# An attention and token-mixing kernel whose instruction order is written out: one sign operation for the first batch, V's sums on either engine, a third buffer of maxima and a new order

## The chip, the cores and the metric

The kernel runs on one core of one Trainium2 chip. The metric is the device time of one execution in microseconds (us), the median of three runs. A core has five engines with a queue of instructions each: TensorE (PE, its weight loads shown as PEld), VectorE (DVE), ScalarE (ACT), GpSimd (POOL) and SyncE (SP), which here only issues DMAs. An engine works its queue off in order and waits on semaphores for the others.

## What is computed

```python
def _attn_ref(q, k, v, proj):                 # 4 batches, 8 heads, 768 tokens, 64 wide
    q_bits = (np.einsum('bhsd,dk->bhsk', q, proj) > 0)      # 6 signs a token
    k_bits = (np.einsum('bhsd,dk->bhsk', k, proj) > 0)
    mask = bucket(q_bits)[:, :, :, None] == bucket(k_bits)[:, :, None, :]
    scores = np.where(mask, 0.125 * q @ k.T, -1e9)
    attn = np.exp(scores - scores.max(-1, keepdims=True))
    attn = attn / (attn.sum(-1, keepdims=True) + 1e-09)
    return attn @ v

def _moe_ref(x, w_theta, w_tok_r, w_tok_i, w_ch):           # x: heads side by side, 512 wide
    theta = x @ w_theta
    y = w_tok_r @ (x * cos(theta)) + w_tok_i @ (x * sin(theta))     # mixes the 768 tokens
    u = x + y
    return u + np.maximum(u @ w_ch, 0.0)
```

## The kernel before

**Precision.** Almost every product is made of two float16 halves (a high part and a rest), so three matmuls stand for one. The halves are made on the chip: a scale, a high part (mostly ACT), a rest (DVE or POOL).

**Attention.** Heads are prepared in pairs (`prep_qk`, `prep_v`) and worked one at a time. For a pair, `squares` sums q's and k's squares on ACT, six short DVE operations make the two scales (`sc`, lines 515 to 520), `high` and `low` make the halves (`hl`, lines 492 and 498). TensorE multiplies the raw q and k with the projection into one PSUM tile `pb`: rows 0 to 63 are q's, 64 to 127 k's. `sign` turns them into the mask's rows (`rows`, line 543), which DMAs (`bitd`, line 620) put beside the halves in one of three operand sets `qk`. For the very first head there are no such DMAs: copies on ACT, DVE, POOL and SP put the pieces into `qk` (lines 556 to 562), and the first products `sq` need the scaled q and k and all four pieces of `rows` there.

A head then takes two passes. `maxima`: products `sq` (6 tiles of 128 queries), their row maxima on DVE (`mc`, line 660), joined (`mx`), turned by TensorE (`pmx`) and put as one more row of the operands by a DMA of SP (`row`, line 695), with a flag row (`fl` to `ft`, line 700). `step`: products `st` with that row, exp on ACT (`pf`, line 752), a float16 part (`p`, ACT line 758 or POOL line 760) and its rest (POOL, line 764), then the product with V (`po`), a reciprocal and a scaling into `x` (line 824). Eight of the odd heads of batches 2 and 3 take the other way (`turned`: `bt`, `bm`, `late`) with no maxima pass. Odd head 1 of a pair in batch 0 multiplies V in float32 (`vw`).

`prep_v` loads V (`vb`), makes its halves `vv`, and needs the mean of V over all tokens: POOL adds six slices of `vb` into one (lines 401 and 405), and one float32 matmul with a matrix of 1/768 (`mean`) makes the mean in PSUM.

**Token mixing.** `moe` runs for each batch beside the next batch's attention: `ps_th` (theta), cos and sin on ACT, `f` and the halves `z` on DVE, ACT and POOL, `py` (products with the token weights `wtk`), `u`, `ps_r` (the channel product), a ReLU and a final sum (line 1221). The weights are loaded, split and turned on the way (`wf_t`, `wf_th`, `wf_ch`).

**Order.** Nothing is scheduled when the kernel is built. Each step is an `Op` with the engines it may run on (`alts`) and the buffers it takes (`Slot`); two tables written out in the source, `ORDER` (one token for each step: a letter for the engine, P, A, D, G, S, and the step's number) and `SLOTS` (which of a kind's buffers), fix engine, sequence and buffer. A planner outside the kernel made them. The durations in the `alts` and the constants such as `QK0` were the planner's and have no effect here. `beat` (22 steps of two matmuls `pw`) are matmuls without use.

The pool `mc` of row maxima has two buffers. `mc`, `mx`, the row and the flag row of one head share its number. A turned head holds one of these buffers for its own maxima `bm`.

Of the kernel before, what the change touches and what calls it, by code (L numbers as in the profile page):

```python
# [32 lines left out]
def lsh_attention_moe_kernel(ctx: ExitStack, tc: tile.TileContext, q, k, v, proj, w_theta, w_tok_r, w_tok_i, w_ch, out):  # L33
# [6 lines left out]
    P = 128  # L40
# [64 lines left out]
    FREE = dict(ft=2, mc=2, hl=2, rows=2, sc=2, nat=2, vv=2, x=2, z0=1, z1=1, wx=1, wz=1, wf=1, xt=2, xd=2, vw=2, **BUFS)  # L105
# [150 lines left out]
    def prep_weight(src, dst, nm, n, tag, stage, prio, step, by=1.0):  # L256
# [94 lines left out]
    def prep_v(b, hp, prio):  # L351
        t = {}
        full = t["full"] = [b == 0 and (hp, j) in FULL for j in range(2)]
        onpe = False
# [45 lines left out]
        def s1():  # L400
            POOL.tensor_tensor(t["vb"][:, :, 0:3], t["vb"][:, :, 0:3], t["vb"][:, :, 3:6], ALU.add)

        def s2():
            for n in (1, 2):
                POOL.tensor_tensor(t["vb"][:, :, 0], t["vb"][:, :, 0], t["vb"][:, :, n], ALU.add)

        def mean():
            t["pm"] = pm = bank(sm_, [33, 2, D], f"pm_{b}_{hp}")
            if onpe:
                first = True  # L410
                for j in range(2):
                    if full[j]:
                        for n in range(T):
                            mm(pm[:, j], ones1, t["vw"][j][:, n, :D], first, n == T - 1)
                            first = False
                if n_:
                    js = slice(lo_, lo_ + n_)
                    for n in range(2 * T):
                        c0 = 0 if n < T else W1
                        mm(pm[:, js], one33, t["vv"][:, js, n % T, c0 : c0 + D], first, n == 2 * T - 1)  # L420
                        first = False
            else:
                mm(pm, ones33, t["vb"][:, :, 0], True, True)

        def by(r):
            return 1.0 / S if onpe else sc[r]

        def mh():
            t["mh"] = ap_.tile([33, 2, D], F16, tag=f"mh{sv.idx}", bufs=1, name=f"mh_{b}_{hp}")
# [15 lines left out]
        if not onpe:  # L445
            c = op("va1", prio, on("POOL", 970, s1), [c], [svb])
            c = op("va2", prio, on("POOL", 936, s2), [c], [svb])
        d = op("vmean", prio, on("PE", sum(700 if f_ else 380 for f_ in full) if onpe else 220, mean), [c], [svb, sv, sm_] + sw_)
# [184 lines left out]
    def maxima(h, n_, b, G, asm, own=False):  # L633
# [37 lines left out]
        for blk, (lo, hi) in {1: (4, 6), 0: (0, 4)}.items() if own else ((0, (0, T)),):  # L671
            def group(blk=blk, lo=lo, hi=hi):
# [3 lines left out]
                def small(nm_):  # L676
                    return ap_.tile([hi - lo, P], F16, tag=f"{nm_}{lo}_{hi}{smc.tag}", bufs=1, name=f"{nm_}_{nm}_{lo}")
# [638 lines left out]
FOURTHS = ()  # L1316
# [24 lines left out]
    "0000000000000000000000101012021202122001300010000011100100110020001010101103110002111111222033301001011033212201103003130110020311"  # L1341
    "1200111031011101010100011100101010111011132002201003031111030332022010111203032031100131203011010000000033000110011030011001111131"
    "1232103201211010303321211102001031332002021101001311120011101101130000100011130010101001131131100120011113030232020313200332101111"
    "3100311130011020310000000321011000101101111001010010123101000133201131021030012130032112103000103213000213012102320320111300010111"
    "2101010010000111101101010010011313010011213123201200211010113321023020130332112310011010023201031321101010003000021010000011000111"
    "0100012101013123200101323010102320120100113131332112200332010300201132120303201011011131011300111010100111001011013010032013213201"
    "0031000022313320300011101030103203201211102311321011022303000001200013111100011031102331133211000323021101000232102303111001000310"
    "0101200112321023031121110030000111110133010010111020112331111120012230311112300110200133200033032111212102233010121003000013312000"
    "1100010110101011101030030000133200110100123103120323110010121012001033101302110220013103103001111011011311110001111012001112312321"
    "1110132122310000311012200003323111220013003000131102312110220100020003211010110113112222013330200112203000122031102331000000330210"  # L1350
    "0200111112301023011312200201111103101110101001100000233003010110113313221301103301120320101031321031121132200102131003320110211000"
    "3000231101100100210033303010212132011331312012300300201001332101012331001300120120112011031201110210101110001111020022311030000113"
    "1213230030100302330103120112311020101122131300010113221001330010300120103001201030012220111212120111011301222012021031110200011200"
    "0102102001111022011010220211022011022001130110111120012101002011300000001131001211201101003012210102202100030211223002010102111211"
# [206 lines left out]
```

## Time and profile before

| what | value |
|---|---|
| median of 3 runs | 692.23 us (690.75 to 699.36) |
| profiled execution | 687.36 us, its span 685.6 us |
| clock of TensorE granted over the span | 0.999 of full speed |
| busy: PE, PEld | 659.5 us (96%), 389.7 us (57%) |
| busy: DVE, ACT, POOL | 579.1 us (84%), 535.8 us (78%), 457.7 us (67%) |
| DMA | 95.39 MB, mean 139 GB/s |

The profiled execution was shorter than each of the three timed runs; 1.8 us of it lie outside the span. A busy share is a mean over stages: until about 250 us the preparation of weights and of two batches' operands lies beside the attention, after that the mixing's matmuls do.

### The profile page before, as it was taken

The numbers are of one execution on the slowest core, as the hardware profiler recorded it, in microseconds if no ns is written. First come the engines' busy times: TensorE is split into PE (matmuls) and PEld (weight loads), VectorE is DVE, ScalarE is ACT, GpSimd is POOL, SyncE is SP. The second block draws the span as 40 slices with busy tenths as digits, with TensorE's granted clock in tenths as the row PEclk, the third lists the DMA queues.
The fourth block names the chain that finished last, engine by engine and source line by source line (L and its number), as shares of the span: only waits on it lengthen the run. The fifth ranks groups of instructions, "written<-read, shape, count | busy, mean of one in ns | idle before, by whom it ended". The sixth has DMA issues, their size and how long they took to land.

```text
span 685.6 us, 16806 instructions
## 1 busy us (share of the span) xinstructions
PE 659.5 (96%) x6257; PEld 389.7 (57%) x6257; DVE 579.1 (84%) x1236; ACT 535.8 (78%) x947; POOL 457.7 (67%) x453
## 2 busy tenths in 40 slices
PE   7899989899989999999999999999999999999997
PEld 2487776745544556656445565655645565644454
DVE  6999999999999999899988788889978778688121
ACT  5779989999977799999887889998984588873002
POOL 6838857378537668999568778978755898743012
PEclk9999999999999999999999999999999999999999
DMA  6564867677266452579537788989754685880113
GB/s 242 142 170 130 206 165 199 188 156 175 77 170 157 97 111 68 130 197 177 113 82 139 152 167 172 181 210 189 119 105 62 138 173 103 139 177 17 32 29 109
DMA packets 176985, 95.39 MB, mean 139 GB/s; under 512 B 149024, under 2 KB 166792, under 8 KB 176904
## 3 DMA queue, kind: packets, MB, share of 16 engines
q1 hardware_dynamic: 176760, 94.30, 61.4%
q8 instruction: 49, 0.80, 0.5%
q14 instruction: 32, 0.26, 0.2%
q10 hardware_dynamic: 144, 0.03, 0.0%
HBM read 32.53 MB, written 6.29 MB: 57 GB/s over the span
## 4 chain that ended last, share of the span: by engine, by line
PE 64%; DVE 23%; issue 5%; DMA 4%; ACT 2%; POOL 1%; SPq 0%; POOLq 0%; DVEq 0%; ACTq 0%
PE py L82 19%; PE po L82 13%; PE st L82 9%; PE ps_r L82 7%; DVE mc L660 6%; PE ps_th L82 6%; PE sq L82 4%; PE bt L82 4%; DVE f L1164 2%; DMA qk<-row 2%; DVE hl L498 1%; PE pb L82 1%; DVE z L1175 1%; DVE wf_t L244 1%; DVE wf_t L326 1%
## 5 line engine op out<-in xcount | busy, mean ns | idle before, releaser
L764 POOL TENSOR_TENSOR p<-pf,p 128x512 f16<-128x512 f32 x180 | 233.1, 1309 | 73.3 <-ACT p L758 62.9
L82 PE MATMUL py<-z,wtk 128*128 128x512 f16 (+1 forms) x900 | 206.6, 370 | 0.4 <-DVE mt L434 0.2
L660 DVE TENSOR_REDUCE mc<-sq 128x1 f32<-128x512 f32 (+1 forms) x216 | 143.2, 681 | 19.5 <-PE sq L82 18.3
L752 ACT ACTIVATE pf<-st 128x512 f32<-128x512 f32 x216 | 124.9, 592 | 22.0 <-PE st L82 17.5
L82 PEld LDWEIGHTS <-qk 108*128 108x128 f16 (+2 forms) x1056 | 96.1, 99 | 77.7 <-issue 17.7
L82 PEld LDWEIGHTS <-wtk 128*128 128x128 f16 x900 | 85.6, 97 | 89.8 <-issue 3.7
L82 PE MATMUL st<-qk 108*128 108x256 f16 (+1 forms) x576 | 124.9, 326 | 3.9 <-DMA qk<-row 2.3
L918 POOL TENSOR_TENSOR late<-pf,late 128x384 f16<-128x384 f32 x96 | 93.2, 985 | 25.2 <-ACT late L912 20.5
L82 PEld LDWEIGHTS <-p 128*128 128x128 f16 x2160 | 85.7, 97 | 21.5 <-issue 2.5
L758 ACT ACTIVATE p<-pf 128x512 f16<-128x512 f32 x148 | 90.7, 626 | 6.7 <-PE po L82 5.6
L82 PE MATMUL po<-vv,p 128*128 128x65 f16 (+1 forms) x2160 | 93.3, 193 | 0.1
L82 PE MATMUL sq<-qk 108*128 108x256 f16 (+1 forms) x288 | 78.5, 325 | 8.3 <-DVE mc L660 4.0
L904 ACT ACTIVATE pf<-bt,bm 128x384 f32<-128x384 f32 x96 | 60.7, 665 | 21.1 <-DVE bm L892 16.8
L82 PE MATMUL ps_th<-wth,t_x 128*128 128x512 f16 x288 | 68.2, 379 | 1.4 <-DVE z L1130 0.8
L82 PE MATMUL ps_r<-wch,t_u 128*128 128x512 f16 x276 | 68.9, 379 | 0.3 <-DVE wch L298 0.3
L876 DVE TENSOR_REDUCE bm<-bt 128x1 f32<-128x384 f32 x96 | 50.4, 549 | 11.2 <-PE bt L82 10.6
L1218 ACT ACTIVATE rl<-ps_r,qu 128x512 f32<-128x512 f32 x23 | 15.7, 683 | 46.8 <-PE ps_r L82 37.2
L82 PEld LDWEIGHTS <-t_x 128*128 128x128 f16 x288 | 27.4, 97 | 33.0 <-DMA t_x<-s_x 1.8
L1221 POOL TENSOR_TENSOR x<-rl,x 128x512 f32<-128x512 f32 (+1 forms) x9 | 12.0, 1328 | 48.2 <-DVE s_u L1020 32.7
L82 PE MATMUL bt<-qk 108*128 108x384 f16 x192 | 43.3, 327 | 0.0
L82 PEld LDWEIGHTS <-t_u 128*128 128x128 f16 x276 | 25.4, 97 | 26.8 <-issue 1.6
L1164 DVE SCALAR_TENSOR_TENSOR f<-x,zsc,z 128x512 f32<-128x512 f32 x48 | 38.8, 833 | 1.2 <-POOL z L1175 1.1
(177 smaller groups left out, 1084.0 us busy)
## 6 DMA issues: line engine op xcount, KB each, us to landing
qk<-hl SPq DMA_DIRECT2D x62, 192.0 KB
raw<-in_q_dram SPq DMA_DIRECT2D x16, 384.0 KB
raw<-in_k_dram SPq DMA_DIRECT2D x16, 384.0 KB
vb<-in_v_dram SPq DMA_DIRECT2D x16, 384.0 KB
qk<-hl SPq DMA_DIRECT2D x62, 96.0 KB
out_dram<-x SPq DMA_DIRECT2D x23, 256.0 KB
w_t<-in_moe_w_tok_r_dram SPq DMA_DIRECT2D x6, 768.0 KB
w_t<-in_moe_w_tok_i_dram SPq DMA_DIRECT2D x6, 768.0 KB
```

Source lines behind the costliest of these rows:

```text
L82: PE.matmul(out_, l, r, start=start, stop=stop, skip_group_check=True)
L244: return lambda: eng.tensor_tensor(t["f"][:, part], t["f"][:, part], t["sg"][:, part], ALU.mult)
L660: DVE.tensor_reduce(col()[:, cs], u["sq"], AX.X, ALU.max)
L752: ACT.activation(wide("pf", spf, F32), u["st"], AF.Exp, scale=1.0 / (UNIT * math.sqrt(D)))
L758: ACT.activation(o_, u["pf"], AF.Copy)
L764: return lambda: eng.tensor_tensor(wide("p2", sp2, F16), u["pf"], u["p1"], ALU.subtract)
L876: DVE.tensor_reduce(part(y), w["w"], AX.X, ALU.max)
L904: ACT.activation(w["f"], w["w"], AF.Exp, bias=part(4), scale=part(3))
L918: return lambda: eng.tensor_tensor(dst(1), w["f"], dst(0), ALU.subtract)
L1164: DVE.scalar_tensor_tensor(u["f"], tl[b][:, tt], zsc[:, b : b + 1], t["zw"][r][:, tt], ALU.mult, ALU.mult)
L1218: ACT.activation(v_["r"][:, ds_], r_["ps"][:, ds_], AF.Relu, scale=t["qu"][:, to : to + 1])
L1221: return lambda: eng.tensor_tensor(tl[b][:, to, ds_], v_["r"][:, ds_], tl[b][:, to, ds_], ALU.add)
```

## The change

- `FOURTHS = (0,)`: in batch 0 `sign` is one DVE operation on 128 partitions in place of two on 64. The `rows` tile then holds q's and k's rows below each other, and the copies to the operand sets take four DMAs of 12 rows (`bits`, line 595 of the new kernel) in place of two that took q's and k's together (`pairs`).
- V's sums are one step with two choices: POOL as before, or one `tensor_reduce` on DVE over the six slices into a tile `va` of its own. The new `ORDER` takes DVE for 10 of the 16 pairs.
- A third buffer for the maxima (`mc=3`). The small row tiles of the first head share their buffers with the later ones of the same number; `mh` has one buffer in place of two.
- The sums over a weight matrix (`total`) multiply with bfloat16 ones in place of float32 ones (two matmuls of one column).
- `ones` and `one33`, which nothing needs any more, and code for another way of V's mean that was never taken are gone.
- `ORDER` and `SLOTS` are new. Both orders hold the same matmuls, but for the two above. The planner's own assumption on the length of weight loads and its random shifts stand in no line of the kernel but these tables.

```diff
-    FREE = dict(ft=2, mc=2, hl=2, rows=2, sc=2, nat=2, vv=2, x=2, z0=1, z1=1, wx=1, wz=1, wf=1, xt=2, xd=2, vw=2, **BUFS)
+    FREE = dict(ft=2, mc=3, hl=2, rows=2, sc=2, nat=2, vv=2, x=2, z0=1, z1=1, wx=1, wz=1, wf=1, xt=2, xd=2, vw=2, **BUFS)
...
-            mm(u["pa"], ones, col, True, True)
+            mm(u["pa"], onesb, col.bitcast(BF16)[:, 1:2], True, True)
...
-        def s1():
+        def sums():
             POOL.tensor_tensor(t["vb"][:, :, 0:3], t["vb"][:, :, 0:3], t["vb"][:, :, 3:6], ALU.add)
-
-        def s2():
             for n in (1, 2):
                 POOL.tensor_tensor(t["vb"][:, :, 0], t["vb"][:, :, 0], t["vb"][:, :, n], ALU.add)
 
+        def reduced():
+            t["va"] = ap_.tile([P, 2, D], F32, tag="va" + svb.tag, bufs=1, name=f"va_{b}_{hp}")
+            DVE.tensor_reduce(t["va"], t["vb"].rearrange("p h t d -> p h d t"), AX.X, ALU.add)
+
...
-                mm(pm, ones33, t["vb"][:, :, 0], True, True)
+            mm(pm, ones33, t["va"] if "va" in t else t["vb"][:, :, 0], True, True)
...
-            t["mh"] = ap_.tile([33, 2, D], F16, tag=f"mh{sv.idx}", bufs=1, name=f"mh_{b}_{hp}")
+            t["mh"] = ap_.tile([33, 2, D], F16, tag="mh", bufs=1, name=f"mh_{b}_{hp}")
...
-            c = op("va1", prio, on("POOL", 970, s1), [c], [svb])
-            c = op("va2", prio, on("POOL", 936, s2), [c], [svb])
+        c = op("va", prio, {"POOL": (1906, sums), "DVE": (860, reduced)}, [c], [svb])
...
-                    return ap_.tile([hi - lo, P], F16, tag=f"{nm_}{lo}_{hi}{smc.tag}", bufs=1, name=f"{nm_}_{nm}_{lo}")
+                    return ap_.tile([hi - lo, P], F16, tag=f"{nm_}{lo}{smc.tag}", bufs=1, name=f"{nm_}_{nm}_{lo}")
...
-FOURTHS = ()
+FOURTHS = (0,)
...
-S66 S68 P0 So P3 Am S3c Pg S6t Pb A67 Dn P6k A69 D6a D6b Pj D6l P4 P2 D6c S6q A6o Pd G6n D6d D6e D6f Ph D6s S6r A6g Pi Pe D6p A6i P9 D6h Pf
+S68 S66 Pl S6t S3c Pb Am So P3 Pi Dn A69 P6k A67 A6u D6a P2 D6b D6c D6d D6e D6f D6l P6v A6i Pj D6s P1 S86 A6g Pa G6n D6w D6r Pe G6q A6m D6x
```

How the start of the program stands in two queues. ACT's rows from its first squares to the last copy for the first head, before (`raw` are q and k, `vb` is V, `qk` the first operand set; lines 487 and 380 are squares, 492 the high parts, 558 copies):

```order
L487 ACTIVATE hl_0_176,sc_0_177<-raw_0_0_155 128x768
L487 ACTIVATE hl_0_176,sc_0_177<-raw_0_0_157 128x768
L558 ACTIVATE qk_141<-rows_0_191 12x384
L492 ACTIVATE hl_0_176<-raw_0_0_155,sc_0_177 128x768
L492 ACTIVATE hl_0_176<-raw_0_0_157,sc_0_177 128x768
L558 ACTIVATE qk_141<-raw_0_0_155,sc_0_177 64x768
L380 ACTIVATE vv_121,vs_0_227<-vb_0_172 128x12x64
```

The same of ACT now:

```order
L467 ACTIVATE hl_0_174,sc_0_175<-raw_0_0_151 128x768
L467 ACTIVATE hl_0_174,sc_0_175<-raw_0_0_153 128x768
L374 ACTIVATE vv_117,vs_0_183<-vb_0_158 128x12x64
L472 ACTIVATE hl_0_174<-raw_0_0_151,sc_0_175 128x768
L472 ACTIVATE hl_0_174<-raw_0_0_153,sc_0_175 128x768
L538 ACTIVATE qk_137<-raw_0_0_153,sc_0_175 64x768
L538 ACTIVATE qk_137<-raw_0_0_151,sc_0_175 64x768
L538 ACTIVATE qk_137<-hl_0_174 64x768
```

The copy of `rows` has left ACT, V's squares stand before the high parts, and both scaled copies of 64 rows are here now. SP's first loads go with it: V's is the third now and was the sixth.

DVE's rows from the scales of q and k to the first maxima, before:

```order
L515 TENSOR_SCALAR sc_0_177<-sc_0_177 128x1
L516 RECIPROCAL sc_0_177<-sc_0_177 128x1
L543 TENSOR_SCALAR rows_0_191<-pb_0_181,pp 64x384 x2
L517 TENSOR_SCALAR sc_0_177<-sc_0_177 128x1
L518 TENSOR_SCALAR sc_0_177<-sc_0_177 128x1
L519 TENSOR_SCALAR sc_0_177<-sc_0_177 128x1
L520 TENSOR_SCALAR sc_0_177<-sc_0_177 128x2
L562 TENSOR_SCALAR qk_141<-raw_0_0_157,sc_0_177 32x768
L562 TENSOR_SCALAR qk_141<-raw_0_0_157,sc_0_177 64x768
```

The same of DVE now:

```order
L495 TENSOR_SCALAR sc_0_175<-sc_0_175 128x1
L496 RECIPROCAL sc_0_175<-sc_0_175 128x1
L497 TENSOR_SCALAR sc_0_175<-sc_0_175 128x1
L498 TENSOR_SCALAR sc_0_175<-sc_0_175 128x1
L499 TENSOR_SCALAR sc_0_175<-sc_0_175 128x1
L500 TENSOR_SCALAR sc_0_175<-sc_0_175 128x2
L523 TENSOR_SCALAR rows_0_193<-pb_0_177,pp 128x384
L542 TENSOR_SCALAR qk_137<-raw_0_0_151,sc_0_175 32x768
L190 TENSOR_SCALAR vsc<-pa_0_195 128x1
L540 COPY qk_137<-rows_0_193 12x384
```

The scales stand before the signs now; the signs are one row in place of two, and the 64-row copy has gone to ACT.

SP's rows around the second head's row of maxima in batch 0 (head 1), before:

```order
L606 DMA qk_143<-hl_1_279 64x2x768
L607 DMA qk_143<-hl_1_279 64x2x768
L609 DMA qk_143<-hl_1_279 32x2x768 x2
L620 DMA qk_143<-rows_1_475 12x2x384 x2
L695 DMA qk_142<-row_1_0_561 1x6x128
L700 DMA ft_86<-fl_1_0_563 1x6x128 x2
```

The same place of SP now:

```order
L586 DMA qk_139<-hl_1_284 64x2x768
L587 DMA qk_139<-hl_1_284 64x2x768
L589 DMA qk_139<-hl_1_284 32x2x768 x2
L595 DMA qk_139<-rows_1_358 12x384 x4
L675 DMA qk_138<-row_1_0_551 1x6x128
L680 DMA ft_86<-fl_1_0_560 1x6x128 x2
```

Ahead of the row of maxima (line 675) stand four issues for the signs, which were two. This is so seven times in batch 0.

## Rows read from the trace of the kernel before

**Rows 1.** The page: part 1 (busy, instructions), part 4 (chain by engine).

```profile
PE 659.5 (96%) x6257; PEld 389.7 (57%) x6257; DVE 579.1 (84%) x1236; ACT 535.8 (78%) x947; POOL 457.7 (67%) x453
PE 64%; DVE 23%; issue 5%; DMA 4%; ACT 2%; POOL 1%; SPq 0%; POOLq 0%; DVEq 0%; ACTq 0%
```

**Rows 2.** Busy time by stretch: stretch, its length, engines (instructions), clock, DMA share, GB/s.

```profile
0.00:25.00 25.00, 19.78 (x123) 8.78 (x124) 18.56 (x52) 14.84 (x26) 17.44 (x41) 1.00 0.64 205
25.00:125.00 100.00, 94.93 (x1000) 70.68 (x996) 96.06 (x204) 87.65 (x162) 65.39 (x60) 1.00 0.64 165
125.00:250.00 125.00, 116.97 (x1076) 66.19 (x1076) 123.34 (x235) 109.82 (x196) 80.07 (x63) 1.00 0.60 147
250.00:660.00 410.00, 406.52 (x3917) 229.82 (x3916) 333.67 (x735) 319.25 (x560) 288.82 (x286) 1.00 0.64 129
660.00:686.00 26.00, 21.26 (x150) 14.18 (x147) 7.43 (x14) 4.25 (x8) 5.98 (x5) 0.97 0.33 91
```

**Rows 3.** The chain that ended last: start, length, what.

```profile
618.58 23.96 PE py L82 x111
```

**Rows 4.** Timeline of the first 14 us: start, length, engine, line, operation, what it waited for.

```profile
3.08 0.48 SPq L368 DMA_DIRECT2D vb<-in_v_dram  x1
...
5.83 0.19 ACT L487 ACTIVATION_READ_ACCUMULATOR hl<-raw 128x1 f32 x1
...
6.19 1.39 DVE L543 TENSOR_SCALAR rows<-pb,pp 64x384 f16<-64x384 f32 x2 [0.75 <-PE pb L82]
...
7.60 1.71 SPq L556 DMA_DIRECT2D qk<-rows  x2
7.61 0.21 DVE L517 TENSOR_SCALAR sc<-sc 128x1 f32<-128x1 f32 x1
...
7.96 0.50 POOL L560 COPY qk<-rows 12x384 f16<-12x384 f16 x1
...
8.23 0.25 DVE L520 TENSOR_SCALAR sc<-sc 128x2 f32<-128x2 f32 x1
8.52 1.76 ACT L492 ACTIVATE hl<-raw,sc 128x768 f16<-128x768 f32 x2 [1.10 <-DVE sc L520]
...
10.18 0.92 ACT L558 ACTIVATE qk<-raw,sc 64x768 f16<-64x768 f32 x1
...
12.51 0.87 ACT L380 ACTIVATE vv<-vb 128x768 f16<-128x768 f32 x1 [1.41 <-DMA vb<-in_v_dram]
...
12.98 0.59 PE L82 MATMUL sq<-qk 108*128 108x256 f16 x3 [2.90 <-DMA qk<-rows]
...
13.40 1.89 DVE L660 TENSOR_REDUCE mc<-sq 128x2 f32<-128x512 f32 x3 [1.78 <-PE sq L82]
```

**Rows 5.** Groups by line and shape: busy, mean ns | idle before.

```profile
L660 DVE TENSOR_REDUCE mc<-sq 128x1 f32<-128x512 f32 x144 | 96.9, 682 | 12.6 <-PE sq L82 11.7
...
L876 DVE TENSOR_REDUCE bm<-bt 128x1 f32<-128x384 f32 x96 | 50.4, 549 | 11.2 <-PE bt L82 10.6
...
L543 DVE TENSOR_SCALAR rows<-pb,pp 64x384 f16<-64x384 f32 x32 | 21.5, 672 | 1.0 <-PE pb L82 0.7
...
L1221 DVE TENSOR_TENSOR x<-rl,x 128x512 f32<-128x512 f32 x15 | 12.5, 834 | 1.0 <-ACT rl L1218 1.0
...
L244 DVE TENSOR_TENSOR wf_t<-wf_t 128x768 f32<-128x768 f32 x10 | 11.7, 1175 | 0.0
...
L1133 DVE TENSOR_SCALAR z<-z 128x512 uint32<-128x512 uint32 x8 | 4.0, 499 | 0.1
...
L250 DVE TENSOR_TENSOR wf_ch<-wf_ch,wg_ch 128x256 f32<-128x256 f32 x6 | 2.8, 462 | 0.0
```

**Rows 6.** ACT's float16 part of exp, same view.

```profile
L758 ACT ACTIVATE p<-pf 128x512 f16<-128x512 f32 x148 | 90.7, 626 | 6.7 <-PE po L82 5.6
```

**Rows 7.** Waits of PE: who waited for whom, us in total, times, longest.

```profile
PE st L82 <- DMA qk<-row: 2.3, 3, 1.9
```

**Rows 8.** Tile `rows`, its DMA issues: min/median/max ns, first and last start.

```profile
L620 SPq DMA_DIRECT2D qk<-rows x62: 779/828/1472, 12.1 to 566.5; - x62
```

More of the change, by code (lines that the diff above doesn't have):

```diff
@@ L398, in low @@
             DVE.scalar_tensor_tensor(t["vf"][:, hs_, W1 : W1 + D], src()[:, hs_], sc, t["vf"][:, hs_, :D], ALU.mult, ALU.subtract)
-        def s1():
+        def sums():
             POOL.tensor_tensor(t["vb"][:, :, 0:3], t["vb"][:, :, 0:3], t["vb"][:, :, 3:6], ALU.add)
-        def s2():
             for n in (1, 2):
                 POOL.tensor_tensor(t["vb"][:, :, 0], t["vb"][:, :, 0], t["vb"][:, :, n], ALU.add)
+        def reduced():
+            t["va"] = ap_.tile([P, 2, D], F32, tag="va" + svb.tag, bufs=1, name=f"va_{b}_{hp}")
+            DVE.tensor_reduce(t["va"], t["vb"].rearrange("p h t d -> p h d t"), AX.X, ALU.add)
         def mean():
             t["pm"] = pm = bank(sm_, [33, 2, D], f"pm_{b}_{hp}")
[L409 to L422, printed above, removed]
-                mm(pm, ones33, t["vb"][:, :, 0], True, True)
+            mm(pm, ones33, t["va"] if "va" in t else t["vb"][:, :, 0], True, True)
         def by(r):
-            return 1.0 / S if onpe else sc[r]
+            return sc[r]
         def mh():
-            t["mh"] = ap_.tile([33, 2, D], F16, tag=f"mh{sv.idx}", bufs=1, name=f"mh_{b}_{hp}")
+            t["mh"] = ap_.tile([33, 2, D], F16, tag="mh", bufs=1, name=f"mh_{b}_{hp}")
             ACT.activation(t["mh"], t["pm"], AF.Copy, scale=by(slice(0, 33)))
@@ L444, in prep_v @@
         c = last_
-        if not onpe:
-            c = op("va1", prio, on("POOL", 970, s1), [c], [svb])
-            c = op("va2", prio, on("POOL", 936, s2), [c], [svb])
-        d = op("vmean", prio, on("PE", sum(700 if f_ else 380 for f_ in full) if onpe else 220, mean), [c], [svb, sv, sm_] + sw_)
+        c = op("va", prio, {"POOL": (1906, sums), "DVE": (860, reduced)}, [c], [svb])
+        d = op("vmean", prio, on("PE", 220, mean), [c], [svb, sv, sm_] + sw_)
         f = op("vmh", prio, on("ACT", 500, mh), [d], [sm_, sv])
@@ L1345 @@
[L1345 to L1348, printed above, removed]
@@ new lines @@
+    "0222113030331001212201103123100120320112020013100203111001111101103100011011001010011101000020331312110301311220123103120120000301"
+    "0131013110013020010003000111201010011211000010001101311201132032010310313112002020331101203310110012310223011200000131131212231110"
+    "0101121100101001311211011000000001003121121113002031220001201311303101211231011213030120003112121303012000011000001001100011010110"
+    "1011000002111010312201032120101130202102113300202210310102111312310013030211310320011111012002011111103000001100110112021031310311"
@@ new lines @@
+    "2201231030210130131032013022021310310120100213131031020201130001000003110010100000022331100013121323033111000213003213210013000012"
+    "1021101012020113031001110130200111010110121101000131013200021030003320021132112021130101311112323002303011202003111112030102313000"
+    "1100012101000100130100200012120311211212130300211130111202131001100022003323013221013222010010011111013001110000003102120123111231"
+    "3000131030012231012103100103232101101001002100230013313002111100030002312010110111011323003001021023213211222131300001131110332331"
@@ L1497 @@
+S33t A351 P361 A35z G352 P362 D360 P363 P364 S353 P365 P366 A369 P367 P368 D36a A36c D36d S36b S36e
 """
```

298 lines of the change are left out of this document (143 added, 155 removed).

## The prediction

> **What bounds the kernel now.** I read the page's busy shares first, then its chain, then the busy time by stretch, then the timeline of the start. The page says that TensorE is busy for 96% of the span and that the chain that ended last runs 64% over TensorE and 23% over VectorE [rows 1]. The reader is to see that these are two stages and not a mixture. From 250 to 660 us TensorE is busy for 406.52 of 410 us and VectorE for 333.67: TensorE is the bound, and all its idle time there is 3.5 us [rows 2]. From 25 to 250 us VectorE is busy for 96.06 of 100 and 123.34 of 125 us, that is 219.4 of 225, while TensorE lacks 5.1 and 8.0 us, 13.1 in all [rows 2]: here TensorE waits for maxima, halves and weights that VectorE makes. In the first 25 us VectorE is busy for 18.56, and the first useful products start only at 12.98 us; what TensorE does before is beats [rows 2, 4].
>
> Both orders hold the same matmuls (all but two, of one column). So time can only come out of waits: 13 us between 25 and 250, some 4 after 250, and the start. That is the frame for everything below.
>
> **Whether TensorE is full after 250 us.** In the last batch 111 matmuls of 512 columns follow each other in 23.96 us of the chain, 0.216 us each, with nothing in between [rows 3]; I take such a stretch as full. The Trainium skill (Perfetto Trace Analysis, Identifying the Most-Contended Engine) calls matmul busy time a bad metric of the distance to the roofline and wants the weight loads' busy share in its place. By that rule the stage has 44% to spare, as PEld is busy for 229.82 of 410 us, and a new order could take far more than 3.5 us there; by the row it can't. What that would give is the last rival.
>
> **The change, part by part.** The sum is made against the profiled execution of 687.36 us; the median of the three runs lies 4.9 us above it, and I carry the difference over to the median unchanged.
>
> *The start.* Before, the two sign operations (1.39 us) stood between the second and the third of the six scale operations on VectorE: signs from 6.19, scales done at 8.48; then ACT's two high parts (1.76) and its scaled copy (0.92) ended at 11.10, and one copy of `rows` went through an SP DMA issued second in a pair of 1.71 us from 7.60 on, so that `sq` started at 12.98, after a wait for that DMA [rows 4]. Now the six scale operations follow ACT's second sum, which ends at 6.02 [rows 4]. From the start of the third, 7.61, to the end of the last, 8.48, four took 0.87 [rows 4], so six take 1.3: scales at 7.3. Signs at 8.0 (one operation of 0.67; 384 elements of each partition as before, so I take the same duration for 128 partitions as for 64 [rows 5]). Three of the four copies of `rows` are on POOL, 0.50 each [rows 4], done by 9.6; the fourth is a short one on VectorE. On ACT V's squares come first (0.87 and an accumulator read of 0.19 [rows 4]). Is V there? Three loads of 128x768 float32, 0.39 MB each, at the 205 GB/s of the first 25 us [rows 2] take 5.8 us, so it lands at about 6.5, an estimate that lets the transfers begin 0.7 us into the span; ACT is free of V at 7.55, the high parts end at 9.3, two scaled copies of 0.92 end at 11.1. That, and no longer the DMA, is the last thing `sq` waits for: 11.1 in place of 12.98. VectorE's halves (two of about 1 us from 9.3) end as the first maxima arrive, so nothing stands before them. Gain 1.9 us. Bounds: if V came only where ACT found it before, at 12.51 [rows 4], ACT's queue would stand still behind its squares and `sq` would start at 17: a loss of 4 us. With V at once, a gain of 2.1. I take 1.9, since V was the sixth load and is the third.
>
> *VectorE's work in the stage that it bounds.* I count its instructions in both orders up to the last scaling into `x` of batch 1, where the stage is over. Signs: 20 operations of 64 partitions become 12 and 4 of 128, four fewer of 0.672, minus 2.7 us [rows 5]. V's sums: five of the 10 that VectorE takes over lie there. No row shows a reduction over 768 elements from SBUF; 384 took 0.549 and 512 took 0.682 us [rows 5], a straight line through them gives 0.95. Bounds are 0.68 and the 1.175 of a product over 768 elements [rows 5]; I take 0.95, so plus 4.75 (3.4 to 5.9). Steps that go from VectorE to another engine or past that point: three weight products of 0.462, one of 1.175, two magnitudes of 0.499 and one final sum of 0.834, minus 4.4 [rows 5]; the rest, of both signs and each under 0.7, is plus 0.9. Sum: minus 1.4 us. As VectorE is the bound there, I count 1.3 as time. So what the signs give, the sums take back almost twice, and only the steps handed to other engines leave something.
>
> *POOL and ACT.* POOL is let off five sums in that stage and gets other work; it is busy for 145.5 of 225 us there [rows 2], so this is worth nothing. ACT gets more: up to the last exp of batch 0's last head 6.8 us more, 3.1 of it five more float16 parts of 0.626 [rows 6]. I cost it at nothing: ACT idles for 27.5 us from 25 to 250 [rows 2]. If that cover is gone, see the first rival.
>
> *The third buffer of maxima.* The waits of `sq` for maxima are over PSUM tiles, which stay two; no row names a wait for `mc`. Zero; at best it lets the order remove VectorE's idle time of 5.6 us between 25 and 250 [rows 2].
>
> *Signs by four DMAs.* Seven times two more issues of 0.83 us on SP [rows 8], 11.6 us, ahead of the row of maxima. Zero, as TensorE waited for that row for 2.3 us in all [rows 7]; second rival.
>
> *The rest.* The bfloat16 column, one buffer of `mh` and the shared small tiles: under 0.5 us either way, taken as zero. After 250 us and at the end the order has 3.5 us to win and as much to lose; zero. What is late next when the start comes earlier is VectorE itself, so the gain stays.
>
> **Sum:** 687.36 minus 1.9 minus 1.3 gives 684.2, in terms of the median 692.23 minus 3.2, **689.0 us**. A difference of about 2% (14 us) is what a measurement of this kernel can tell from none, and this is far inside it. Its own range is 686 to 691.5.
>
> **The rivals.**
> 1. *ACT takes VectorE's place; the gain is given back.* ACT is busy for 109.82 of 125 us from 125 to 250 and for 87.65 of 100 before [rows 2]. Of its 6.8 us more, 3.7 fall between the last exps of heads 3 and 7. For: exp stands between `st` and everything behind it, and a float16 part put on ACT delays the exps queued behind it on ACT, and POOL, which waits for that part. Against: ACT idled for 12.4 us from 25 to 125 [rows 2]. If it costs as much as the start and VectorE give, the time is 692, range 691 to 695. It holds if ACT's idle time from 25 to 125 falls under 8 us and TensorE's stays at 5 or more.
> 2. *The slower side: SP's queue.* In batch 0 four issues for signs (3.3 us in place of 1.7) stand ahead of the row without which `st` can't start. TensorE waited for that row three times, 2.3 us [rows 7]. If each of the seven adds its 1.66 us to the path, 11.6 us: 689.0 plus 11.6 is 700.6; with half of them 694.8. It decides from the point where SP is still issuing when the row has been made. Against: the sign rows are asked for a head earlier than the row, and most waits for it were none.
> 3. *The order wins more.* Maxima in a third buffer let VectorE run on: its 5.6 us of idle time go as well. 689.0 minus 5.6 is 683.4.
> 4. *TensorE isn't full.* If a tenth of the 180 us in which no weights are loaded after 250 us (410 minus 229.82 [rows 2]) came out, 18 us: 671. The page named above speaks for it, the 0.216 us spacing against it [rows 3].
>
> **How the numbers follow.** Forecast 0.50, rival 1 0.24, rival 2 0.15, rival 3 0.09, rival 4 0.02. Likeliest: 689.0. The range for 8 in 10 takes in rival 3 and half of rival 2 and the bounds of V's landing and of the reduction: 681 to 698. Faster by over 2% (under 678.4) needs rival 4 or all of rival 3 and luck after it: 0.04. Slower by over 2% (over 706) needs rival 2 in full and rival 1 or V's late landing on top: 0.04. Within: 0.92.
>
> **What would show it.** V's squares on ACT at 6.4 to 6.6 us and the first `sq` at about 11.1, released by ACT's copy; first maxima at 11.5; the reduction `va` at 0.95 us; VectorE still busy for over 97% from 25 to 250 us; the last scaling of batch 1 some 3 us earlier; from there on TensorE idle for no more than 4 us up to the last 25. Wrong would be: a start at 11 with batch 1's end where it was (rival 1, if ACT is full; rival 2, if `st` waits for the row), or an end that differs though batch 1's doesn't (the order after 250 us).

## The result and the profile after

The changed kernel takes 697.41 us (median of 20 runs, 693.48 to 702.5); the kernel before 691.8 (20 runs). The ratio is 1.0087, interval 1.0063 to 1.011: about 6 us slower, where 3.2 us faster was forecast. The range of 681 to 698 holds it. The profiled execution took 697.41 us, its span 695.6, at a granted clock of 0.991.

Of the kernel before, the profile caught an execution that is shorter (687.36 us) than all twenty timed ones, so the two spans differ by 10.0 us and the medians by under 6: some 4 us of what the stages below add up to are chance. (Executions of one kernel spread with the clock that TensorE is granted: of 29 of the kernel before, timed on one chip beside later runs, the nine at 0.988 or less took 696.1 us or more, and the eleven at 0.996 or more took 693.1 or less.)

The page of the changed kernel, parts 1 and 4, against [rows 1]:

```profile
PE 665.0 (96%) x6255; PEld 392.0 (56%) x6255; DVE 597.1 (86%) x1228; ACT 528.4 (76%) x929; POOL 452.0 (65%) x453
PE 52%; DVE 19%; issue 2%; ACT 2%; POOL 0%; DVEq 0%; ACTq 0%; POOLq 0%
```

The shares read as before; VectorE has 18 us more in eight fewer instructions. Where it lies is in the stages, to be held against [rows 2]:

```profile
0.00:25.00 25.00, 17.36 (x87) 7.09 (x87) 18.20 (x50) 16.11 (x27) 15.35 (x38) 1.00 0.64 210
25.00:125.00 100.00, 95.23 (x988) 68.89 (x988) 91.39 (x193) 83.41 (x156) 61.12 (x55) 0.97 0.60 163
125.00:250.00 125.00, 114.54 (x1019) 66.63 (x1020) 122.51 (x214) 107.88 (x188) 71.00 (x60) 0.99 0.58 143
250.00:660.00 410.00, 406.24 (x3967) 230.49 (x3965) 357.92 (x759) 316.00 (x551) 299.49 (x299) 1.00 0.65 131
660.00:696.00 36.00, 31.65 (x198) 18.90 (x195) 7.06 (x13) 5.05 (x9) 5.07 (x4) 0.97 0.28 66
```

The third stage is as full as it was. The loss lies ahead of it: from 25 to 125 us VectorE is busy for 91.39 us, which was 96.06, and the granted clock is 0.97. Batch 0's last scaling into `x` ends at 140.42 us (134.29 before), batch 1's at 311.74 (300.04), batch 3's at 617.50 (607.50). So between the two profiled executions 6 us are lost in batch 0, nearly 6 in batch 1, and 2 come back later.

The first loss is one gap. The timeline of the changed kernel around 22 us (start, length, engine, line, operation, what it waited for):

```profile
21.67 1.03 PE L77 MATMUL pw<-ft 128*128 128x512 f16 x4
...
22.73 1.20 SPq L680 DMA_DIRECT2D ft<-fl  x2
...
25.88 1.01 PE L77 MATMUL pw<-ft 128*128 128x512 f16 x2 [3.19 <-DMA ft<-fl]
26.95 0.61 PE L77 MATMUL st<-qk 108*128 108x512 f16 x1
```

`pw` is a beat: two matmuls whose result nobody reads. But its operand is the tile `ft`, into which the flag rows of a head are copied. In the new order the last beat stands behind head 0's second flag row, so TensorE's queue stops for 3.19 us until that copy has landed, with the products `st` behind it. In the kernel before, the last beat stood ahead of that copy:

```profile
22.32 0.59 PE L82 MATMUL pw<-ft 128*128 128x512 f16 x2
...
22.95 1.20 SPq L700 DMA_DIRECT2D ft<-fl  x2
```

What follows in the changed kernel, in stretches of 5 us (columns as above), and one stretch of the kernel before:

```profile
20.00:25.00 5.00, 2.69 (x17) 1.19 (x14) 4.14 (x13) 3.75 (x7) 2.64 (x4) 0.99 0.37 105
25.00:30.00 5.00, 4.06 (x18) 1.53 (x19) 1.29 (x2) 1.32 (x3) 1.24 (x2) 0.50 0.94 276
30.00:35.00 5.00, 4.81 (x50) 2.91 (x48) 3.64 (x6) 3.93 (x7) 3.24 (x4) 0.83 0.05 10
```

```profile
25.00:30.00 5.00, 3.85 (x18) 1.35 (x14) 4.95 (x9) 4.15 (x9) 4.92 (x6) 1.00 0.86 243
```

Behind the gap TensorE is granted 0.50, the lower of its two levels (1.2 of 2.4 GHz), until past 30 us, and VectorE is busy for 1.29 us of 5, where it was for 4.95. The engine that bounds this stage has run dry.

The second loss lies beside more work on VectorE. Up to batch 1's last scaling, the kernel before and then the changed one:

```profile
0.00:300.04 300.04, 281.24 (x2800) 177.21 (x2801) 283.50 (x584) 258.83 (x466) 205.45 (x201) 1.00 0.60 153
```

```profile
0.00:311.74 311.74, 287.16 (x2802) 179.22 (x2803) 290.53 (x577) 262.08 (x470) 195.14 (x191) 0.98 0.57 147
```

Of the 11.7 us between these ends VectorE is busy for 7.0 more and idle for 4.7 more; that idle time is all there by the end of batch 0 (15.6 against 10.4 us). TensorE, in turn, is busy for 5.9 us more with the same matmuls (2802 records against 2800): half of the 11.7 us is matmuls that last longer, at a mean granted clock of 0.98. Part of that lies at the gap above, part at 145 us, behind a wait of 2.09 us for VectorE's maxima at 144:

```profile
145.00:150.00 5.00, 4.77 (x31) 2.83 (x30) 5.00 (x7) 3.25 (x4) 5.00 (x4) 0.72 0.83 172
```

V's sum and two of VectorE's groups that grew, in the changed kernel and then, without the sum, in the one before:

```profile
L392 DVE SCALAR_TENSOR_TENSOR vv<-vb,vsc,vv 128x768 f16<-128x768 f32 x12 | 15.0, 1253 | 0.3 <-ACT vv L388 0.2
L401 DVE TENSOR_REDUCE va<-vb 128x128 f32<-128x768 f32 x10 | 14.9, 1491 | 0.0
...
L226 DVE SCALAR_TENSOR_TENSOR wf_ch<-w_ch,wf_ch 128x256 uint32<-128x256 uint32 x8 | 6.9, 858 | 0.1
```

```profile
L398 DVE SCALAR_TENSOR_TENSOR vv<-vb,vsc,vv 128x768 f16<-128x768 f32 x12 | 13.3, 1110 | 0.1
...
L231 DVE SCALAR_TENSOR_TENSOR wf_ch<-w_ch,wf_ch 128x256 uint32<-128x256 uint32 x8 | 5.1, 633 | 0.1
```

V's sum `va` takes 1.49 us. The other two are the same work as before, 1253 ns for 1110 and 858 for 633. Other groups became shorter: eight rests `z`, up to batch 1's end, took 8.06 us in all and take 5.60.

The start, which was to win 1.9 us:

```profile
1.69 0.43 SPq L362 DMA_DIRECT2D vb<-in_v_dram  x1
...
8.21 0.87 ACT L374 ACTIVATE vv<-vb 128x768 f16<-128x768 f32 x1 [2.33 <-DMA vb<-in_v_dram]
...
9.07 1.74 ACT L472 ACTIVATE hl<-raw,sc 128x768 f16<-128x768 f32 x2
...
10.72 1.75 ACT L538 ACTIVATE qk<-raw,sc 64x768 f16<-64x768 f32 x2
...
12.52 0.60 PE L77 MATMUL sq<-qk 108*128 108x512 f16 x3 [0.53 <-ACT qk L538]
```

ScalarE's steps last what the prediction took for them, in its sequence, and the first products are released by its copy. But V lands at 8.2 us, 6.5 after its issue, and ScalarE's queue stands still for 2.33. The products start 0.46 us earlier than before [rows 4].

### The profile page after: what moved, and what is told of

The parts are those of the page before. It is cut to its first block, busy times and chain, and to the rows that moved or that the text cites. A ratio compares the mean times of both kernels' runs of the same rounds, so it can differ in the third digit from the quotient of the medians.

```text
span 695.6 us, 16757 instructions
## 1 busy us (share of the span) xinstructions
PE 665.0 (96%) x6255; PEld 392.0 (56%) x6255; DVE 597.1 (86%) x1228; ACT 528.4 (76%) x929; POOL 452.0 (65%) x453
## 4 chain that ended last, share of the span: by engine, by line
PE 52%; DVE 19%; issue 2%; ACT 2%; POOL 0%; DVEq 0%; ACTq 0%; POOLq 0%
PE py L77 20%; PE po L77 8%; PE ps_r L77 6%; PE st L77 5%; PE ps_th L77 5%; DVE mc L640 4%; PE bt L77 4%; PE sq L77 2%; DVE hl L478 1%; DVE bm L856 1%; DVE f L1144 1%; DVE x L1186 1%; DVE rows L523 1%; DVE va L401 1%; DVE vv L392 1%
## 5 line engine op out<-in xcount | busy, mean ns | idle before, releaser
L744 POOL TENSOR_TENSOR p<-pf,p 128x512 f16<-128x512 f32 x180 | 229.3, 1286 | 84.2 <-ACT p L738 71.2
L77 PE MATMUL st<-qk 108*128 108x512 f16 (+1 forms) x576 | 126.5, 331 | 2.8 <-ACT pf L732 2.1
L898 POOL TENSOR_TENSOR late<-pf,late 128x384 f16<-128x384 f32 x96 | 97.1, 1023 | 20.5 <-ACT late L892 15.5
L738 ACT ACTIVATE p<-pf 128x512 f16<-128x512 f32 x140 | 85.9, 625 | 10.8 <-PE po L77 9.2
L77 PE MATMUL sq<-qk 108*128 108x256 f16 (+1 forms) x288 | 80.4, 329 | 10.1 <-DVE mc L640 8.5
L77 PE MATMUL ps_r<-wch,t_u 128*128 128x512 f16 x276 | 70.7, 379 | 0.3 <-DVE x L1186 0.3
L1198 ACT ACTIVATE rl<-ps_r,qu 128x512 f32<-128x512 f32 x23 | 15.6, 679 | 41.8 <-PE ps_r L77 40.3
L1201 POOL TENSOR_TENSOR x<-rl,x 128x512 f32<-128x512 f32 x11 | 14.8, 1348 | 45.6 <-ACT rl L1198 45.6
L1144 DVE SCALAR_TENSOR_TENSOR f<-x,zsc,z 128x512 f32<-128x512 f32 x48 | 41.2, 875 | 2.3 <-POOL z L1155 1.2
L1186 DVE SCALAR_TENSOR_TENSOR x<-py,sw,x 128x512 f32<-128x512 f32 x23 | 17.1, 744 | 27.6 <-PE py L77 27.5
```

What stands on the lines that cost most here:

```text
L77: PE.matmul(out_, l, r, start=start, stop=stop, skip_group_check=True)
L738: ACT.activation(o_, u["pf"], AF.Copy)
L744: return lambda: eng.tensor_tensor(wide("p2", sp2, F16), u["pf"], u["p1"], ALU.subtract)
L898: return lambda: eng.tensor_tensor(dst(1), w["f"], dst(0), ALU.subtract)
L1144: DVE.scalar_tensor_tensor(u["f"], tl[b][:, tt], zsc[:, b : b + 1], t["zw"][r][:, tt], ALU.mult, ALU.mult)
L1186: DVE.scalar_tensor_tensor(tl[b][:, to], res["py"], t["sw"][:, to : to + 1], tl[b][:, to], ALU.mult, ALU.add)
```

## The experiments

Three theories. **A**: TensorE's wait for the flag row, and what follows it. **B**: VectorE's work, in the sums of V and in instructions that last longer beside GpSimd. **C**: SP's additional sign copies, the prediction's second rival. Each kernel is given by its ratio to the kernel before, timed on the same chip, with its interval. Two experiments are compared by these ratios, and they ran on three chips (e1 to e4 on one, e5 to e11 and m1 on a second, e12 to e15 on a third); where one is called faster or slower than another, the two intervals part, mostly by only 0.1%.

**The flag row behind the beat (e1).** One token of `ORDER` moves. Every engine keeps its sequence; only now the copy waits for the beat.

```diff
-P8 Ab9 S7y Dbc Pc P9f
+P8 Ab9 Dbc Pc S7y P9f
```

> The changed kernel with one entry of the order moved: the flag row of head 0 is issued behind the last beat and not ahead of it; no engine's own sequence changes, only which of the two waits. Theory A (TensorE's wait at 22.3 us for that flag row, 3.35 us, and the granted clock of 0.50 and 0.83 in the ten us behind it, cost about half of the loss): the wait shrinks to under 1 us, the clock from 25 to 35 us is 1.00, batch 0 ends about 5 us earlier (135.4 in place of 140.4), the time falls by 5 us to 692.4. Theory B (VectorE: the sums of V at 1.48 us and its instructions longer beside GpSimd cost it all): no change, 697, as VectorE is just as full behind. Theory C (SP's sign copies): no change.

1.0016 (0.998 to 1.0053), which lies wholly under the changed kernel's interval: 0.71% or 4.9 us less. Its timeline at the place, and the stretches behind it:

```profile
21.74 1.46 PE L77 MATMUL pw<-ft 128*128 128x512 f16 x6
23.23 1.20 SPq L680 DMA_DIRECT2D ft<-fl  x2
...
23.26 0.61 PE L77 MATMUL st<-qk 108*128 108x512 f16 x2
```

```profile
20.00:25.00 5.00, 4.94 (x39) 2.47 (x38) 4.79 (x15) 4.53 (x9) 2.64 (x4) 1.00 0.38 111
25.00:30.00 5.00, 4.81 (x65) 3.05 (x61) 5.00 (x9) 4.91 (x11) 5.00 (x6) 1.00 0.79 210
```

`st` follows the beats at once, 3.7 us earlier, VectorE is full and the clock stays at 1.00. Theory A holds for most of the loss, though the two intervals part by only 0.1%. (The profiled execution is one of 699.32 us, the slowest of this kernel's twelve, median 693.75: at 100 us TensorE stood for 1.6 us in it and was granted 0.50 for some 6 us behind. So the end of its batch 0, which the expectation names, can't be compared.)

**V's sums by additions (e2).** In `reduced`:

```diff
...
-            DVE.tensor_reduce(t["va"], t["vb"].rearrange("p h t d -> p h d t"), AX.X, ALU.add)
...
+            DVE.tensor_tensor(vb[:, :, 0:3], vb[:, :, 0:3], vb[:, :, 3:6], ALU.add)
+            for n in (1, 2):
+                DVE.tensor_tensor(vb[:, :, 0], vb[:, :, 0], vb[:, :, n], ALU.add)
```

> The changed kernel with V's sums on VectorE made by three additions over contiguous slices (384, 128 and 128 elements) in place of one reduction that steps 64 elements at a time. By the rows of the trace (1.175 us for a product of 768 elements, 0.46 for 256) the three should take 0.9 to 1.1 us in place of 1.48. Theory B: five of them lie in the stage that VectorE bounds, so minus 2 to 3 us, 695. Theory A and C: no change, 697.

1.0186 (1.0138 to 1.0233): 7 us slower than the changed kernel, against the expectation. The additions took 0.77 us (384 elements) and twice 0.84 (128 elements), 2.46 in place of 1.49. My price for an addition was wrong; the measurement m1 below tells why. Where the 7 us lie is another matter. Five of the ten sums stand up to batch 1's end, which comes at 313.94 us in place of 311.74, 2.2 later for 4.8 us more of sums. The rest comes from there to batch 3's last scaling, in the changed kernel and then in this one:

```profile
311.74:617.50 305.76, 304.39 (x3067) 175.14 (x3065) 271.67 (x598) 245.55 (x430) 243.13 (x250) 1.00 0.74 146
```

```profile
313.94:624.56 310.62, 304.46 (x3063) 174.86 (x3062) 276.47 (x608) 245.55 (x430) 244.40 (x250) 1.00 0.72 143
```

Here TensorE is the bound and VectorE has slack, and yet TensorE is idle for 6.2 us and not for 1.4. So longer sums cost time, but most of it outside the stage that theory B speaks of; it is no proof of that theory.

**V's sums on GpSimd (e3)**, the letter D of ten tokens turned into G:

```diff
-Dbn Dth Dyb D135 D17z D1df D1ob D1tr D1z7 D24n
+Gbn Gth Gyb G135 G17z G1df G1ob G1tr G1z7 G24n
```

> The changed kernel with all sixteen sums of V on GpSimd, as before the change; the rest of the order stays. Theory B in the form that the sums' own time counts: 7.4 us less on VectorE in its stage, 690 to 691. Theory B in the form that GpSimd's work makes VectorE's instructions longer: part is given back, 694 to 697, and the mean of VectorE's other instructions rises. Theory A: no change, 697.

1.0119 (1.0067 to 1.0172), not to be told from the changed kernel. VectorE is busy for 5.2 us less up to the end of batch 1 and not 7.4, idle for 3.5 more, and batch 1 ends 1.8 us earlier; by the end of batch 3 this is gone. Moving the sums back wins nothing, so work taken off VectorE isn't time one for one.

**The signs in two operations (e4)**, `FOURTHS = ()` in the changed kernel:

> The changed kernel with the signs of batch 0 made by two operations of 64 partitions again and brought by two copies (the first batch's special case off). Theory B: VectorE has 2.7 us more to do (four operations of 0.67), 700. Theory C (four issues of SP ahead of the row of maxima hold up the products): 5.8 to 11 us faster, 686 to 691. Theory A: as theory B, or no change if VectorE has slack.

1.0109 (1.0063 to 1.0155): not faster. Theory C doesn't explain the changed kernel.

**The wait put into the kernel before (e5).** Its last beat, P1, moves behind the flag row S7z.

> The kernel before, with its last beat moved behind the second half's flag row of head 0 and behind the product that follows it, so that TensorE waits there as the changed kernel does. Theory A: TensorE stands from 23.4 us until the flag row has landed at about 26, 2.5 us; VectorE runs dry and the granted clock falls behind it; 3 to 5 us slower than the kernel before, 695 to 697. Theory B and C, or that VectorE has slack enough to hide it: no change, 692.

1.0026 (0.9986 to 1.0065). TensorE now waits for the flag row for 3.4 us in that kernel, but the time isn't to be told from no change, nor from the 3 us that were expected. It doesn't decide.

**The signs in one operation, in the kernel before (e6)**, `FOURTHS = (0,)` alone:

> The kernel before with the signs of batch 0 in one operation of 128 partitions and four copies of 12 rows; nothing else of the change. Theory B: VectorE has 2.7 us less to do, 689. Theory C (four issues of SP ahead of the row of maxima): 3 to 11 us slower, 695 to 703. If signs don't matter: 692.

1.0078 (1.0032 to 1.0123), 5.4 us slower. Here theory C's mechanism is at work. The row of maxima that the kernel before issues at 81.06 us, and its product (first fence), and the same two with four sign copies (second):

```profile
81.06 0.72 SPq L695 DMA_DIRECT2D qk<-row  x1
```

```profile
87.43 0.81 PE L82 MATMUL st<-qk 98*128 98x512 f16 x3 [1.88 <-DMA qk<-row]
```

```profile
74.35 3.47 SPq L615 DMA_DIRECT2D qk<-rows  x4
...
83.21 0.72 SPq L695 DMA_DIRECT2D qk<-row  x1
...
90.31 1.44 PE L82 MATMUL st<-qk 98*128 98x512 f16 x3 [3.67 <-DMA qk<-row]
```

The copies take 3.47 us of SP where they took 1.74, the row is issued 2.15 later, and TensorE waits for 3.67 in place of 1.88; 0.50 is granted behind it. In the changed kernel the same product waits for its row for 0.52 us.

**V's squares late (e7)**, on top of e1: on ScalarE behind the copies (A6p), TensorE's and VectorE's steps for V's scale behind the first products.

```diff
-A69 P6k A67 A6u D6a ... P6v ... D6w ... D6x
+A69 P6k A67 D6a ... A6p A6u ... P7j P6v D7k D6w D6x
```

> The kernel of e1 with V's squares moved on ScalarE behind the first head's copies, and the sum over partitions and V's scale behind the first products. In the changed kernel ScalarE stood still for 2.33 us until V landed at 8.2, so the first products should start at about 10.9 in place of 12.5. Theory: this carries through to the end of the stage, 1.6 us less than e1. Rival: what stands at 18 us (the first row of maxima, made by VectorE) or VectorE's work behind it sets the pace, no change against e1.

0.999 (0.9959 to 1.0022), level with the kernel before. The products start at 10.85 us:

```profile
10.71 0.85 ACT L374 ACTIVATE vv<-vb 128x768 f16<-128x768 f32 x1
10.85 0.59 PE L77 MATMUL sq<-qk 108*128 108x512 f16 x3 [0.39 <-ACT qk L538]
```

That is 1.67 us earlier, and 0.26% less than e1; the two intervals overlap.

**The sums measured alone (m1)**, behind the end of the changed kernel:

> The changed kernel with a measurement behind its end: on VectorE six reductions with steps of 64 elements as in V's sums, six over adjacent elements of the same number, six rests of 768 elements, six additions of 128, first with GpSimd idle and then eight of each with GpSimd adding 512 elements at a time beside them. If the steps make the sum slow: 1.48 with steps, 0.85 to 0.95 without. If a reduction of 768 elements is that slow in itself: 1.48 both. If GpSimd beside it makes VectorE slow: the rest 1.01 alone and 1.2 to 1.4 beside; the reductions, which read one operand, the same in both.

In order: reductions with steps of 64 elements, reductions over adjacent ones, rests of 768 elements from two tiles, additions of 128; first alone, then beside GpSimd's additions.

```profile
699.32 8.72 DVE L1264 TENSOR_REDUCE ma<-mb 128x128 f32<-128x768 f32 x6
708.07 5.89 DVE L1268 TENSOR_REDUCE ma<-mb 128x128 f32<-128x768 f32 x6
713.88 6.28 DVE L1273 SCALAR_TENSOR_TENSOR mc__11086<-mb,onesb,mc__11086 128x768 f16<-128x768 f32 x6
720.08 1.91 DVE L1277 TENSOR_TENSOR ma<-mb 128x128 f32<-128x128 f32 x6
...
722.44 12.00 DVE L1264 TENSOR_REDUCE ma<-mb 128x128 f32<-128x768 f32 x8 [0.46 <-POOL md L1280]
722.49 52.96 POOL L1282 TENSOR_TENSOR md<-md 128x512 f32<-128x512 f32 x36
734.47 7.87 DVE L1268 TENSOR_REDUCE ma<-mb 128x128 f32<-128x768 f32 x8
742.26 14.65 DVE L1273 SCALAR_TENSOR_TENSOR mc__11086<-mb,onesb,mc__11086 128x768 f16<-128x768 f32 x8
756.83 10.72 DVE L1277 TENSOR_TENSOR ma<-mb 128x128 f32<-128x128 f32 x8
```

By one: 1.45 with steps, 0.98 without, whether GpSimd works (1.50, 0.98) or not. The rest takes 1.05 alone and 1.83 beside GpSimd, the addition 0.32 and 1.34, which is the length of one of GpSimd's additions there. So a reduction, which reads one tile, doesn't mind GpSimd; an instruction that reads two waits for it, and GpSimd waits in turn: its additions take 1.26 each beside the reductions, 1.79 beside the rests and 1.33 beside the short additions.

The Trainium skill (Vector Engine (DVE) Microarchitecture Reference, Measured stream behaviour on trn2) gives, for another instruction, an XOR of two sources, 1.054 ns a column with adjacent reads and 1.73 where one source hops at every element. The reductions here, 1.89 and 1.28 ns an element with their fixed part, differ by nearly as much. The Trainium skill (SBUF — State Buffer, SBUF: two separate sides) says that a VectorE instruction with two SBUF inputs and a GpSimd instruction that reads SBUF hold the shared port pair one at a time, each for its whole length; the addition's 1.34 beside GpSimd's 1.33 agrees.

**V's sums early on GpSimd (e8)**, on top of e7: the first five of the ten tokens.

```diff
-Dbn Dth Dyb D135 D17z
+Gbn Gth Gyb G135 G17z
```

> The kernel of e7 with V's sums of batches 0 and 1 (five of the ten that VectorE had) back on GpSimd; those of batches 2 and 3 stay on VectorE. Theory B: five sums of 1.48 leave the stage that VectorE bounds, 7.4 us of its work; with e3's experience that GpSimd's additions lengthen VectorE's others by 2.2 us and leave 3 us more idle, 2 us of time: 690. If the sums' place doesn't matter: 692, as e7.

1.0006 (0.9972 to 1.0041): no gain over e7. The sums' place doesn't matter, within some 3 us.

**Beats in the gap (e9)**, in the changed kernel: the beat ahead of the waiting one gets 18 matmuls.

```diff
...
-        for _ in range(2):
+        for _ in range(18 if n == 8 else 2):
...
```

> The changed kernel with sixteen more idle matmuls (3.5 us) in the beat just ahead of the one that waits for the flag row. TensorE waits as long as before for useful work but doesn't stand still. If the fall of the granted clock behind the gap costs by itself: clock 1.00 from 20 to 35 us, 2 to 3 us less than the changed kernel, 694 to 695. If only the wait costs: 697, whatever the clock.

1.0068 (1.0029 to 1.0107), and it doesn't decide, as it doesn't fill the gap:

```profile
20.04 4.48 PE L77 MATMUL pw<-ft 128*128 128x512 f16 x20
...
24.55 1.21 SPq L680 DMA_DIRECT2D ft<-fl  x2
...
26.90 0.59 PE L77 MATMUL pw<-ft 128*128 128x512 f16 x2 [2.39 <-DMA ft<-fl]
```

The flag row's copy in turn waits for the beats that read `ft` before it. It is issued when they end, and the last beat waits on.

**The third buffer alone, in the kernel before (e10)**: maxima in three buffers in turn, small tiles merged for the room.

```diff
...
+                if sl.pool == "mc" and sl not in put_:
+                    sl.idx = len(put_) % 3
...
```

> The kernel before with its maxima in three buffers in turn (one tile that nothing reads is gone, and small tiles share a buffer, for the room); the order stays. If no wait goes through these buffers: no change, 692. If VectorE's idle time between 25 and 250 us came from them: up to 5 us faster, 687 to 690.

0.9942 (0.9904 to 0.998): 4 us faster than the kernel before, and the best version of this study.

**Four copies alone, in the kernel before (e11)**: each sign copy of batch 0 cut into q's and k's.

```diff
-                dma(out_[MR:K1, :, 0, x * SH : (x + 1) * SH], t["rows"][r0 : r0 + NM])
...
+                for i in range(2):
+                    dma(out_[MR:K1, i, 0, x * SH : (x + 1) * SH], t["rows"][r0 : r0 + NM, i])
```

> The kernel before with the sign rows of batch 0 brought by four copies in place of two; the sign operations on VectorE stay two. Theory C, as far as e6 showed it (SP issues the row of maxima of a later head 2 us later, and it lands behind weight loads): the same loss as e6, 695 to 698. If e6's loss came from the signs themselves: 692.

1.0063 (1.0016 to 1.011), as e6: in the old order it is SP's issues that cost.

**Do these two act in the new order?** The signs in two operations and two copies, on top of e7 (e12):

> The kernel of e7 (flag row behind the beat, V's squares late) with the signs of batch 0 in two operations and two copies again. If SP's four copies cost in the new order what they cost in the old one (4 us in e11): 688, 0.993 of the kernel before. If they cost nothing there and only VectorE's 2.7 us more count: 695.

1.0068 (1.0033 to 1.0102), 5.4 us slower than e7. On top of e7 the one operation with its four copies is a gain, twice the 2.7 us priced; in e4, the same edit of the changed kernel itself, it was 1.5 us, inside the intervals. Two buffers in turn, on top of e7 (e13):

> The kernel of e7 with its maxima in two buffers in turn in place of three. The order was laid out for three, so a head's first maxima now wait until the maxima of the head but one before are read: if the third buffer carries weight, 3 us or more slower than e7, 695 or more; if not, 692.

1.0061 (1.0031 to 1.0092), 4.9 us slower than e7.

**The control of e10 (e14)**: its merged tiles, but two buffers.

> The control of e10: the kernel before with the same tiles merged and the unread tile gone, but with two buffers of maxima. If the third buffer was the gain of e10: 692, as the kernel before. If the merged tiles or the shifted addresses were: 688 to 690, as e10.

1.0028 (0.9989 to 1.0066): the gain of e10 was the third buffer's, though the intervals only just part.

**V's squares late, with the wait left in (e15):**

> The changed kernel with V's squares late, as in e7, but with the last beat still behind the flag row. If the late squares gain their 1.8 us by themselves: 695.5. If the wait for the flag row swallows them: 697, as the changed kernel.

1.007 (1.0037 to 1.0102). Against the changed kernel this is 1.2 us, inside the intervals; against e7, which differs from it by the flag row alone, 0.8% or 5.5 us. So theory A is shown twice, by e1 and by e7 against e15.

The trace of e15 holds one thing more. The wait is there, and the clock doesn't fall behind it:

```profile
25.17 0.59 PE L77 MATMUL pw<-ft 128*128 128x512 f16 x2 [3.34 <-DMA ft<-fl]
```

```profile
25.00:30.00 5.00, 4.77 (x46) 2.69 (x47) 3.30 (x6) 3.50 (x7) 2.34 (x3) 1.00 0.83 238
```

This execution took 692.63 us, 2.5 under the median of its kernel (695.12).

## Why the prediction was wrong

**The frame** was right in part. Both orders hold the same matmuls, but "time can only come out of waits" left out that the same matmuls last longer at a lower granted clock: 5.9 of the 11.7 us up to batch 1's end. And waits stood in the sum only as something to win; a new wait in TensorE's queue was put at nothing, without a reason. The step that failed is the one that filled this frame: "As VectorE is the bound there, I count 1.3 as time." It compared how much work stands in the two orders, and not what an instruction waits for in its new place; and when e3 took 5.2 us of work off VectorE, no time came of it. The beat behind the flag row isn't in the prediction. Beats were spoken of as what TensorE does before 13 us; that they read `ft`, and that the last of them had come behind a copy into it, stood in the order. It cost 4.9 to 5.5 us of the 6. Without it (e1) the kernel is level with the one before, still some 4 us above the forecast.

**The start** (minus 1.9): it gave 0.46. ScalarE's steps, their sequence and the release by its copy came as said; V's landing at "about 6.5" was 8.2, between the value taken and the bound of 12.51. The loads of three weight matrices, issued from 2.16 us on, were under way beside V's; whether they took its share was not tried. Late squares bring the start to 10.85, and of that 1.2 to 1.8 us show in the time, which the intervals can't tell from none.

**VectorE's work** (minus 1.4): plus 7.0. Counted by kind with the durations of before, the changed set of instructions comes to plus 1.0, with `va` at its own 1.48: the count was right, and the sum was mis-sized, 0.95 for 1.48, beyond its upper bound of 1.175, since the rows that I drew the line through read adjacent elements. The other 6 us are, on balance, the same instructions lasting longer, some of them shorter; the prediction carried each at its old mean. m1 shows a mechanism that can do this, GpSimd beside instructions with two operands. That the new order puts more of them there was not tried, and GpSimd is busy for 10 us less up to that point (195.14 against 205.45). Nor is it shown that the 7.0 us are time: e3 and e8 moved sums away and won nothing.

**The third buffer** (zero): about minus 4 in the old order (e10) and minus 4.9 in the new one (e13 against e7). The waits for PSUM tiles, and that "no row names a wait for `mc`", were no reason to put it at nothing. Its size is near rival 3's 5.6 us, and the losses hid it. That it works as rival 3 said, by letting VectorE run on, is not shown: from 25 to 250 us VectorE is idle for 4.7 us in e10 and 10.7 in its control e14, for 8.3 in e7 and 12.2 in e13, but for 5.6 in the kernel before, which has two buffers too.

**The signs' copies** (zero): the second rival's mechanism is real in the old order (e6, e11: 4.4 to 5.4 us, nearer its half than its whole) and not in the new one, where the product waits for its row for 0.52 us and undoing them, together with the one operation, costs time in e12 and wins none in e4. Rival 1 needed ScalarE's idle time from 25 to 125 us under 8 us; it is 16.6. Rival 4 is out: from 250 to 660 us TensorE is busy for 406.24 of 410 us in the new order as well, though PEld is at 230.49. The section of the Trainium skill that it drew on (Perfetto Trace Analysis, Identifying the Most-Contended Engine) asks for the rate of matmul work beside the weight loads' share; the prediction took the second alone.

**What stays open:** why the signs are worth 5.4 us on top of e7; why V's sums can go to either engine at no price; how much of the flag row's cost is the low clock and how much the wait, which e9 was to part. An estimate from the executions: the mean granted clock is 0.991 in the changed kernel and 0.995 in e1, 0.992 in e15 and 0.997 in e7; in the kernel before, 0.01 of clock goes with some 6 us, so about half of the cost would be the clock's. The parts don't add up to the 6 us, as each depends on the order around it.

## What to carry to other kernels

Instructions without use still have operands: before an order is compared by its work, look at each moved instruction on the engine that must not stop, and ask which copy or engine last wrote what it reads; here one token among thousands, moved by two places, was worth 5 us. Compare medians before the stages of two profiles: each profile is one execution, and here chance made 4 of their 10 us. Price a reduction by how its elements lie, and a VectorE instruction with two SBUF operands by what GpSimd does beside it. The same edit can win in one order and lose in another (the four copies), so measure it in the order that it will run in; and what is best here, the old order with a third buffer of maxima at 0.9942, was found by taking the change apart.

## What the runs showed of the hardware

A reduction over 768 elements with steps of 64 takes 1.45 us, over adjacent ones 0.98. An addition of 128 elements takes 0.32 us alone and 1.34 beside GpSimd's additions, and a rest of 768 elements 1.05 and 1.83, so that of these two the short one suffers more. Three additions for one reduction made V's sum longer, 2.46 for 1.49. Gaps of TensorE of 1.6 us (at 100 us in e1's profile) and of 3.2 us (at 22 us) were each followed by some 5 us or more at a granted clock of 0.50. It is no rule: a gap of 3.34 us at the same place in e15's profile was followed by a clock of 1.00.
